# Conformer block on one core: 56 of 69 chunk transposes by DMA transposes inside SBUF

## The chip, the cores and the metric

The kernel runs on one core of a Trainium2 chip. The metric is the device time of one execution in microseconds (us), the median of several runs. In the text, PE is TensorE (its matmuls; PEld its weight loads), ACT ScalarE, DVE VectorE, POOL GpSimd, and SP the engine that issues most of the DMAs.

## The reference

Two sequences of 4000 tokens, 144 features each, in bfloat16, go through one Conformer block:

```python
def reference(x, w_ff1a, w_ff1b, w_qkv, w_o, w_pw1, dw, w_pw2, w_ff2a, w_ff2b):
    h = _layernorm(x, axis=-1)
    h = _silu(h @ w_ff1a) @ w_ff1b                    # 144 -> 576 -> 144
    x = x + 0.5 * h
    h = _layernorm(x, axis=-1)
    qkv = h @ w_qkv                                   # 4 heads of 36
    ...
    p = _softmax(scores, axis=-1)                     # 4000 x 4000 for each head
    att = jnp.einsum('bhqk,bhkd->bhqd', p, v)
    ...
    x = x + att @ w_o
    h = _layernorm(x, axis=-1)
    h = h @ w_pw1                                     # a, b: 144 each
    h = a * _sigmoid(b)
    ...                                               # depthwise convolution over 5 tokens
    x = x + _silu(c) @ w_pw2
    h = _layernorm(x, axis=-1)
    h = _silu(h @ w_ff2a) @ w_ff2b
    x = x + 0.5 * h
    return _layernorm(x, axis=-1)
```

## The kernel before

The 8000 tokens are cut into 16 chunks of 500, eight for each sequence, and a chunk into four blocks of 125. `X` holds all tokens in SBUF with tokens on the partitions. The attention of a chunk runs over the keys in tiles of 64: PE makes scores from `QT` and `KT` into PSUM, an exponential turns them into `PT`, and PE multiplies `PT` with `VA` into an accumulator. ACT makes 802 exponentials of 128x1000; for 190 further tiles DVE makes the exponential by integer arithmetic (two `PT<-PS` of 128x500 each, then three steps on `PT`).

Beside the attention run the other stages of each chunk: feed-forward 1 (`ff1`), projections to q, k and v (`pre2`), output projection and gate (`post1`), convolution and feed-forward 2 (`post2`). They need the chunk with features on the partitions. The layer norm (`ln`) is computed token by token: `bn_stats` on DVE, a power and four subtract-and-multiply steps on POOL, into a buffer `XN`. The attention's result is put by DVE into a buffer `AN` (`epilogue`). `transp` (and `transp_q` for the projections) brings such a buffer into the transposed `XT` (or `XTQ`), from which PE's matmuls read.

Of these chunk transposes 69 go the long way (`blocks`): DVE transposes all 32x32 blocks of the buffer, seen as pairs of bfloat16 in one float32, in place. SP issues four DMAs that write the buffer to a DRAM tensor `rows`, waits for their landing, and issues two DMAs that read it back so that the blocks come to stand in place (features 0 to 127, then 128 to 143). Because two blocks of tokens travel as a pair, `XN` and `AN` are written interleaved, and the matmuls read `XT` with a step of two elements. 41 of the 69 start from `XN` and go to `XT`, 15 from `AN` to `XT`, and 13 from `XN` to `XTQ`. The first and last chunks, where latency counts, are transposed on PE instead (`calm`).

The order of each engine's instructions is written out: a planner in the kernel walks through all work with fixed costs (the arguments `cost` and `lat`) and gives a first order, `PLACES` says which PSUM banks a tile takes, and `ORDER`, a string for each engine, says by how many places each step is moved from there. `Rec.reorder` applies it; `Rec.finish` works out the semaphore waits. Each engine then works through its own list in order, so an instruction that waits holds up those behind it. SP's list holds the loads of `X`, the stores of the result, and the DMAs of the transposes. All instructions are issued from one helper line, 398, which is why the profile shows that line everywhere.

Of the kernel before, what the change touches and what calls it, by code (L numbers as in the profile page):

```python
# [8 lines left out]
F32 = mybir.dt.float32  # L9
# [30 lines left out]
        "PPPPPPQOQOPPPPPRPNPPQQQQLPPQORPNPRPTMORNNVO~OLNOMrMMNPMMNNNOMNNNOPLMQMMMNNPMMNSMNLMMOOPNSOMQMSPNOPU["  # L40
        "OMNRMOPPQIRMSNPNePNOOOcNNNNNNNNNOOLbNLOOQNSH]MMOLOMPMMOOOVPNOOOOPPPTOOOTPMUQMSLNNQQNQOQQNPPPPPTPPROK"
        "PPPPPPPPPPPP`PPPQKVPPKPPMPPRPUPPPROQQQRZOQQQRRKQRRSJPRRRRRRRWSZRNYUR~NHQ@R[KEGOOOPPPPKQOPPSPPSLPQMTP"
        "PPLQQQMPPPQVPPQOX_PTOPPCRTQQRGSQIQQSQRNV8OOQNNVSNOOLOPUUNN_MMWLNNRMMMMOOOPPPPPPQQNPPRSNRSSSORRVTR[OR"
        "AKQ@PPLOOQQNPPPPPUOOOOOPQOPPPPPUOOOOQRPLU`NNNXMMPNLQMNLZRNL`MN_YLLMK`KMNLILNQJMOOOPNYOPNOOOQNNZ^NNNN"
        "OOPNQNQOYP]CNNNNOMPMSO[NKOOQNVMPMMN`NbYMMMMNOMNIcLLNL[MMMNNQNRMJQLLROQSPLRNOQOPUQOMPQMPPRPVPLQOMQNPQ"
        "QQQSKPQSQKQQQQJPPPPPWQQSPKKQQUPPPSWPQRPQAVPPPQCVPQRPWHSYPHSOPQYPQEPQCPRZUPPSOOHDPR^OKOOOOPNOOOO^NOQN"
        "NOOOSNNNNS[NNNdRMNRKYNJWJNNNNNNGOOPP^YNNNNOMNNNNRNNPPPVROOLOOPPRZNNOOOOOPNOSOPNRPSMOOPQOQWNRPRLLNSZP"
        "NPQOIOQOTPPPRPQ]P^USPMMQIQKQQ8QTQQGMRRTQQKRRRRGLRSOMRPQQQJQQRPVP[OOOQEROO^IOQLNOOPPTTOMNQ[FOQNPPSPPM"
        "HPQOQQUPLOPNVPNOOSQNLUOOPNOXPPPLTQNLMPPPQOPPTOOPTPLOOQRNOPPPQOVPNOOOORZOP[PPMOOFRZOL[ROQKQTUBOKNFPPP"
        "_OOOOOOPNOOOOWNNVNNXMNTKMNOMZQOSLNOMSPSLLTPMOOUOPNOOTQOMOPPPQOPPPQOPPPTTQOSQSSSSNEEPQOPTPTMOMORSNNOP"  # L50
        "ROYPQOPQ^NPNPQOPAOOOOOSOOOPPPQQNPPPPPPXOOOOOOOaNPPPLOOOPUMOOOO[IOOPSOOQNPHPSWOOPPPPQGPPPPQQQMPPQQNPQ"
        "O_OOOPZOOOPI_NNNNZOPEOQWP^HKPHSJOLNOO`VPMRJOM^J`MPNKUNLUGNLJQNRIOPPRXOMOOOOPXMOPPMOOOPWOOPPPTKNOOPPP"
        "PPPPPPPQRPSYSQNQYZPRRRADIOXQGVOPJOORPIPPRRSSMR]MHOOQQQVRKNHPLPPPPPPPPPPRZQSQRRbHSGNQGPPQRRGLPQKQQQQJ"
        "QOQRPMQOPPQOSQNRMTROTNPXQQQEPJOQNPRPN_OPPPLRSOPLPPPGPPPSeOMPPQRJZPKLNNNN`NOKOVJNNNNcM`LMMMNNN]MNL]LL"
        "LLLLTWLXKMMVNQ_LMOPPQQ>MOOOTOMRbMMOOOOOTOOOQZIOPJMOOcOMPPT[PRORPEVHOPYCJQOQQGMOQQNQWNQNPPLSP_OaOOOPN"
        "PDPPPLOHPPQLPPPPQOTPNWNPPPWJNPPP`OIOPPPPPPPUQOELRP^TTQOZUPPCGOPQDJPPPPPPRPQWPRURPMFQQ_RPXDPQJLPNOJPN"
        "PPPPPSPPQ`PPTQQRERPQIQTNDPTPPJOPQQNPPUOPPSLPMPPRPQQRPJP[RNQQLaRJQSS[IQMGQQRPCZJPQOPQTPP@RPIPPPPQQQSS"
        "VXUQGNTQSSETDS`OQSCJQQdLOINQMRLLZMNSMMMMZLWPK]JMNLMTLNNNNVN`NNNNNROOPPJQOPLRPRMOQQRPLPXQQQRPTUQHFPQJ"
        "PPPPPPSPROUSPPTLPUOCOPNQOPROTWPRWRPVRZOY^YEOOPPMQ:;QDQQQQQQQQQEQQQMQOROVSMOTTQLVHROTRGNTVPHRPTRaJSQE"
        "QRSKNRNOQOPWQO=OOPNYOOOQNNOO]QOL_PNRO^NOUIPNK_MMW>MMMZMMMM]MMQLMMSNNOMOPPSOVNNPNXNPQOKQOQLQQQQUPPPHO"  # L60
        "QORPQMQOPQQSQOUVWNWMNOKOAOQOPPPPZWNNNOOLNNR^MNVNOMNNNNPSMN]NTNNNNNaNNNOQLN[RNOMRNHMSOSNPQGPQOPRXRPQW"
        "KOHOPPQYPPZPQRCO[I^NORFNNIZMMMNOWLNNNQMNRORRO_KPNOOOYNNNNNNOU^NSUHNKOJNOSOOQRJUPROTYMHNNURNNTMIPNQOU"
        "OOV[MNLNNNPYTNeJLNORNNGOO[]NNNNIQLMRLNRWOPUOO]OM`QO;LSOLO]JOJPRLLMRUNZMOVR[NPDOT^OOOFOSTOMNOSbPQLPRS"
        "_MORR_NPP^OHCNNNOZOWL~NHLMMNNNSOOXNOQQNSSOIVKPNPN]NOOOOOPPVOOOITNPPLPPQOWPPMRPNTKOOTNOPUMOOOQN`OOOPN"
        "OOPPPLOZOQQMPIQO^YROQQRLENO_PNPPPTQNNOROOSVO]QMNRNOPWTNOMNSOPQXbOOOQ[NO~NCdIMMMMMMMfbKMMMQMMJLMPLMUM"
        "MMNL^TR^JSLJQJUKPNLHQMPP`UNNNNOMOOOOPNOOPPPPQQNPQQQMUQQMSOPTQOPTPQUNQSPSQ<TRSSVEQQQHQQFPPPPPQSPMYTOL"
        "NNTMNNNP^[NOMNNQMMOLNN]PNOOR[OPKQN_ZLNESMOOKHOM[NPPLPNOOPPMQSTMNPQQQQRSQRRTCQVNGRNOMTTTMMNUPPQHNQSPM"
        "YVTQKLLSSOIJPSSPTMKORNOQOPPPPPPSORNSMRNRRRNQQRPFRPQQQQQQRPFQO"
    ),
    "act": (  # L70
        "PPPPPPPPPPPPPRSNNOSOOOPPPPPPPUPNOXNNOOOOOQNPPPPPPPPPROOPPQOPPPQOPPPPPPQQNPPPPPPPPPPPPPPPPPPPPPPPPPQO"
        "PPPPPPPPPPPPPPPPPPPPPPPPPPPPPPPPPPPPPPPPPPPPPPPPPPPPPPPPPPPPPPPPPPPPPPPPQOROSNOOPPPPPPPPPPPPPPPPPPPP"
        "PPPPPPPPPPPPPQOPPPPPPPPPPPPPPPPPPPPPPPPPQOPPQOPPPPPPPPPPPPPPPPPPPPPPPPPPPPPPPPPPPPPPPPPPPPPPPPPPPPPP"
        "PPPPPPPPPPPPPPPPPPPPPPPPPPPPPPPPPPPPPPPPPPPPPPPPPPPPPPPPPPPPPPPPPPPPPPPPPPPPPPPPPPPPPQOPPPPPPPPPPPPP"
        "PPPPPPPPPPPPPPPPPPPPPPPPPPPPPPQOPPQOPPPPPPPPPPPPPPPPPPPPPPPPPPPPPPPPPPPPPPPPPPPPROOPPQOPPPPPPPPPPPPP"
        "PPPPPPPPPPPPPPPPPPQOPPPPPPPPPPPPPPPPPPPPPPPPPQOQOPPPPPPPPPPPPPPPPPPPPPPPPPPPPPPPPPPPPPPPPPPPPPPPPPPP"
        "PPPPPPPPTOPNOPPPPPPPPPPPPPPPPPPPPPPPPPPPPPPPPPPPPPPPPPPPPPPPPPPPPPPPPPPQOPPPPQOPPPPPPPPPPPPPPPPPPPPP"
        "PPPPPPPPPPPPPPPPPPPPPPPPPPPPPPPPPPPPPPPROOPPQQNPPPPPPPPPPPPPPPPPPQOPPPPPPPQOPPPPPPPPPPPPPPPPPPPPPPPP"
        "PPPPPQOPPPPPPPPPPPPPPPPPROOPPPPPPPPPPPPPPPPPQOPPPPPPPPPPPPQOPPPPPPPPPPPPPPPPPPPPPPPPPPPPPPPPPPPPPPPP"
        "PQOPPPPPPPPPPPPQOPPPPPPPPPPPPPPPPPPPPPPPPPPPPPPPPPPPPPPPPPPPPPPPPPPPPPPPPPPQOPPPPPPPPPPPPPPPPPPPPPPP"  # L80
        "PPPPPPPPPPPPPPPPPPPPPPPPPPPPPPPPPQOSPNRNOQOUQNPMOPPPRORNQNPPPPPPQOROQQMPPPPPPQOPPPWORNNNOO"
    ),
    "dve": (
        "PPROQQQLPPPUUNNNNSMUNNPNOQOSPNSUMOPLOPTPNPNPPQQQQQQQQHPVPRPLPLPPPRSSNRNQVPUOODNUMPNPNPPQSPMXNOOQNNOO"
        "PPPPPPPSOOOPPQOPPPPPPPPPPPPPPPPQOQOPPPPPPROQQMQOQOPPQORSQMQQQQQRPQWQRPQLPQQQVQQQSUKTQ2KMPQQQRRORPQQR"
        "RRTQQRTTPP;RPQBPPSOOORPNSOPRPQKQOPPPPPPcPQcQQQQTPPERPDLDNRNRNQQQRFQNQQNQOPQOPPPQOPPPPPPPPPPPPPPPQQTM"
        "PPRPQQQQUQOQUQQQSQRVGPPPPSPPRPQQ/PQOPPSPPQQKPPPPPQOPPPPQOPPPPPROOPQQNROQNPPPPQOPQOQQNPPPQTQOPQRPSPRR"
        "NSPPRPQQQ;QOPPPPPPPPPPPROOQOPSOOOPQOROOUSUOOQSQHRGOPPPPROOPPQRPMQRNQNQOPPPPPPPPPPQOPRPRPQKQOPQQQRPQQ"
        "QQQWROOPQO?PPPPPPPPQOPSOPQePPROOPPEOPNOPNOOOOOQNPPPPPROOPPPPRPRRRRJQKPPQOPPPPPPPPPPPQOPPPYOOPNPRMSMR"
        "LQMPPQOPPPPPPPPPPPPPPPPPQOROOPROOPPPPPPPPQOPQOQOPPROOTOOOOQOSOOOPROQNPPPPPPPPPPPQSPPLQOPPPROOPPPPPPP"  # L90
        "PPPQOPPPPPPPPPPQOPPPPPQOPPPPPPPQQVPLTPMOLPPRPNPQOPPRRNNPROQNPPPPPPPPPPQOQOQORORNOPROOPPPQQNPPPPQOPQR"
        "NOPQOPPPPPSPNOQQNQOPQOPPPPPQQQMPPPPPPPQOPPPQOQRPMROQQMPPQOPSPNOPPUOOOOOWOOOOOOOPPQOPPQQQQRPRPQGPPPPP"
        "PPPPPPQOPPPPUOOOPNPQOSOOSNOSNZQMPLOPNOOOPPPPPPQQNQOQOPPPPQOQOPPPRUOUQOUIOJOOPPPQOPPPPUOOOOOPPPQOROQT"
        "QOPJQOPPPPPPPQQQMPQOPPQRNTNTNNNQNQOPQOROQNPPQOPPPPPPSPNOTOOOOPPPQOQQUPVQOTHPNIQOVOPPMPQMPTOPPRLTNOOO"
        "PPPPPPUOOOOOPQOPPSPSQSQSQUSTEOELQOPPPPPPPSOPNPPROOVOOPNOOPPROOVOOPNOOPQRPUQQQVRUQUPCKPDPPPPQOPPPPQOP"
        "QOQOSPNOhQOPPPPPHOPNOPPQOROQNGOOPPPQOQOPQOPRPNPPPPQOPPPPPROTPPLQRULVOUOJPNJPPQOQOPRPQMPPPPPPPPQQQQQK"
        "QRNRNORPNUOUP[LNKPMRNRNLNQSSMRMRPKQOQQNQOWPPMQOXOPRPNSOWNCPNORNRTTPJSQMSPPQRZOROQQQQTPUHOPRO4PPPPPPQ"
        "QQRLRPQLPPPPPPPPPQOQQQMPPPPPQQQMPPPPPPPPPQQQSLTRPSQJQQQQQRTOPPRPRSQSQRRTQUPQTDO/OPS]NSMOLNQQNLOVQUPU"
        "OKHPLRRNNPPPQOPQRPQQQQVQOPQORSOP?PPPPPPPPPPPPRORPQQRPWQQNPTPUPUKOO<OPQOROQQMPQOPQQNPQQSPTQNPHPPROOQS"
        "NPQULPNOORROQRPJPPSOOORO]SOSNPRWQQXPTRERGRRTTUXRTRSBSSSSSSSSAT@S&NNPPPPPPPPPPQO"  # L100
    ),
    "pool": (
        "PPPPPPRPNPPPROOPPPSOOOPPPPPQQNPQOPPPYOOOOO[NNNR`NNJOMSMMOMOXOOLNOOUORLOMROQQQRPSIOOPPSOOOPQRNOPPPTOO"
        "PNPPPPVOOPNOQNPPPRPQM"
    ),
    "sp": (
        "PPPPPPPPQOPPPPPPPPPPPPPPSOTNNOOPPPQOPPPROQNPPPPPPPPPPPPPQOPPQOQOPPPPPPPPPPPPPPQOPPPPPVOPNSNNQMPPPQOP"
        "ROYNOOOPNOOUNTNOMNPPPSOOOPPPPPPPPPPPPPQOQOPPPPQQN"
    ),
# [16 lines left out]
    "2405240524052020420442045205420524052405240524052042505240524052402505423042302420340342034203420340"  # L126
    "2342042034203420243024202430243024034202340243204303420240240334024204302430243024302340134013413412"
    "0412041201412042041204024012412140214021401241205042304231514236404512412361021452243051351241353250"
    "213024014452502542036410"
)  # L130


# [1973 lines left out]
```

## Time and profile before

| | |
|---|---|
| median of 3 runs | 881.04 us (880.92 to 881.92) |
| span of the profiled execution | 880.5 us |
| the median over that span | 0.54 us |
| PE busy | 851.5 us (97%), 11419 matmuls |
| ACT busy | 849.6 us (96%), 1098 instructions |
| DVE busy | 822.7 us (93%), 1812 instructions |
| POOL busy | 300.4 us (34%), 584 instructions |
| DMA | 28.80 MB; the main queue takes 13.8% of the 16 DMA engines' time |

The profile is of one execution. A group is named by what its instructions write and read, output first (`XT<-rows`); with the number of instructions come their busy time, the mean of one in ns, and the idle time of the engine ahead of them with what ended it. DMA issues stand under SPq. Records of neighbouring instructions of one engine overlap by about 0.07 to 0.2 us, so the time from start to start is shorter than the mean that a group shows.

### The profile page before, as it was taken

The page shows a single profiled execution, that of the slowest core. Times are in us where ns is not written, and L with a number is a line of the kernel's source. Part 1 is how long each engine was busy: PE and PEld are TensorE (multiplying, and loading weights), DVE is VectorE, ACT ScalarE, POOL GpSimd, SP SyncE. Part 2 cuts the span into 40 slices and gives each one's busy share as a digit, 9 for nine tenths or more (in the row PEclk, how much of TensorE's full clock was granted, in tenths as well). Part 3 has the DMA queues.
Part 4 walks back from the last instruction along what each step waited for, and adds up shares of the span by engine and source line. Part 5 has one row for each costly group of instructions (what it writes and reads, how often), then busy time and mean ns, then how long its engine had stood idle before and what let it go on. Part 6 is the DMA issues. An engine that isn't in the chain of part 4 may idle for free.

```text
span 880.5 us, 27000 instructions
## 1 busy us (share of the span) xinstructions
PE 851.5 (97%) x11419; PEld 380.2 (43%) x11419; DVE 822.7 (93%) x1812; ACT 849.6 (96%) x1098; POOL 300.4 (34%) x584
## 2 busy tenths in 40 slices
PE   8998999999999999999999999999999999999996
PEld 6543433344444443443444444344443433444366
DVE  7977999999999999999989999899999999999987
ACT  6799999999999999999999999999999999999986
POOL 7770331431336130252111813522513404032434
PEclk9999999999999999999999999999999999999999
DMA  3221001220221110212001120110110011001111
GB/s 100 44 55 38 16 18 36 62 51 16 40 49 38 23 38 22 45 24 45 16 9 30 36 44 23 23 26 20 43 31 18 21 37 20 17 12 36 27 27 33
DMA packets 114351, 28.80 MB, mean 33 GB/s; under 512 B 101090, under 2 KB 114230, under 8 KB 114230
## 3 DMA queue, kind: packets, MB, share of 16 engines
q1 hardware_dynamic: 112646, 26.39, 13.8%
q8 instruction: 89, 1.46, 0.7%
q10 hardware_dynamic: 1584, 0.69, 0.3%
q14 instruction: 32, 0.26, 0.1%
HBM read 13.44 MB, written 13.61 MB: 31 GB/s over the span
## 4 chain that ended last, share of the span: by engine, by line
ACT 46%; PE 33%; DVE 17%; POOL 2%; DMA 1%; issue 1%; SPq 1%; POOLq 0%; DVEq 0%
ACT PT L398 42%; PE PS L398 33%; DVE PT L398 7%; ACT TH L398 4%; DVE HT L398 2%; DVE ST L398 2%; DVE X L398 2%; DVE XN L398 2%; POOL RS L398 1%; POOL XN L398 1%; DVE KT L398 1%; DVE QT L398 1%; DVE AN L398 1%; SPq L398 1%; DMA rows<-XN 0%
## 5 line engine op out<-in xcount | busy, mean ns | idle before, releaser
L398 ACT ACTIVATE PT<-PS 128x1000 bf16<-128x1000 f32 (+1 forms) x818 | 757.2, 1074 | 4.1 <-PE PS L398 2.4
L398 PE MATMUL PS<-QT,KT 64*64 64x500 bf16 x3968 | 425.7, 385 | 13.0 <-ACT PT L398 5.2
L398 PE MATMUL PS<-PT,VA 64*37 64x500 bf16 x4728 | 411.5, 372 | 1.8 <-DVE QT L398 0.7
L398 DVE TENSOR_SCALAR PT<-PS 128x500 int16<-128x500 f32 x380 | 250.1, 668 | 5.8 <-PE PS L398 3.9
L398 PEld LDWEIGHTS PS<-QT,KT 64*64 64x64 bf16 x3968 | 123.4, 104 | 236.8 <-ACT PT L398 137.1
L398 POOL TENSOR_SCALAR RS<-ST 125x4 f32<-125x4 f32 x130 | 37.0, 284 | 482.2 <-DVE ST L398 475.6
L398 PEld LDWEIGHTS PS<-PT,VA 64*37 64x37 bf16 x4728 | 141.4, 96 | 96.2 <-DVE PT L398 18.7
L398 DVE TENSOR_SCALAR PT<-PT 128x1000 uint16<-128x1000 uint16 x380 | 154.5, 418 | 2.1 <-PE PS L398 0.8
L398 POOL TENSOR_SCALAR XN<-X,RS 125x144 bf16<-125x144 bf16 x260 | 150.4, 610 | 13.1 <-DMA out_dram<-XN 6.4
L398 DVE TENSOR_TENSOR PT<-PT 128x1000 bf16<-128x1000 bf16 x190 | 128.8, 679 | 1.3
L398 ACT ACTIVATE TH<-PS 128x500 bf16<-128x500 f32 (+3 forms) x194 | 107.3, 575 | 7.4 <-PE PS L398 6.5
L398 POOL TENSOR_TENSOR RS<-RS,NHALF 125x4 f32<-125x4 f32 (+1 forms) x93 | 91.7, 989 | 33.1 <-DVE RS L398 27.3
L398 DVE SCALAR_TENSOR_TENSOR HT<-TH,PS 128x500 bf16<-128x500 bf16 (+1 forms) x135 | 81.2, 615 | 12.8 <-ACT TH L398 12.0
L398 PE MATMUL PS<-XT,WA 80*128 80x500 bf16 (+5 forms) x288 | 74.5, 365 | 2.2 <-DMA XT<-rows 0.9
L398 DVE BATCH_NORM_STATS2 ST<-X 125x6 f32<-125x288 bf16 x160 | 65.7, 447 | 2.8 <-DMA X<-in_x_dram 2.7
L398 DVE SCALAR_TENSOR_TENSOR X<-PS,X 125x288 bf16<-125x288 f32 (+1 forms) x128 | 56.6, 449 | 6.5 <-PE PS L398 5.2
L398 PE MATMUL PS<-WB,HT 128*125 128x144 bf16 (+1 forms) x640 | 52.4, 230 | 0.7 <-ACT HT L398 0.5
L398 PEld LDWEIGHTS PS<-WB,HT 128*125 128x125 bf16 (+1 forms) x640 | 44.3, 136 | 14.5 <-issue 3.8
L398 PEld LDWEIGHTS PS<-XT,WA 128*128 128x128 bf16 (+1 forms) x288 | 21.2, 97 | 38.8 <-issue 10.6
L398 PE MATMUL PS<-U,DG 128*128 128x250 bf16 (+6 forms) x204 | 29.6, 264 | 0.0
L398 DVE STREAM_TRANSPOSE XN<-XN 128x320 f32<-128x320 f32 x54 | 27.0, 500 | 1.0 <-POOL XN L398 1.0
L398 POOL COPY U<-U 128x2 bf16<-128x2 bf16 (+1 forms) x54 | 9.2, 209 | 46.3 <-DVE U L398 46.3
(95 smaller groups left out, 522.6 us busy)
## 6 DMA issues: line engine op xcount, KB each, us to landing
rows<-XN SPq DMA_DIRECT2D x216, 40.0 KB, 2.0
XT<-rows SPq DMA_DIRECT2D x56, 128.0 KB, 2.0
rows<-AN SPq DMA_DIRECT2D x60, 40.0 KB, 2.0
X<-in_x_dram SPq DMA_DIRECT2D x15, 140.6 KB
XTQ<-rows SPq DMA_DIRECT2D x26, 70.3 KB
out_dram<-XN SPq DMA_DIRECT2D x13, 140.6 KB
XT<-rows SPq DMA_DIRECT2D x56, 16.0 KB, 1.9
out_dram<-XN SPq DMA_DIRECT2D x3, 70.3 KB
```

The source lines that it names most:

```text
L398: ins = getattr(eng, o.name)(*o.a, **o.k)
```

## The change

For the 56 transposes into `XT`, the block transpose on DVE, the writes to DRAM and the reads back are gone. SP issues four `dma_start_transpose` instead, one for each block of 125 tokens. Each takes 128 partitions by 256 columns of `XN` or `AN` and writes them transposed to 128 partitions by 2x128 in `XT`. A block has 144 columns, so the rest of the 256 are columns of the next blocks; they end in rows of `XT` whose weights are zero. `XN` and `AN` grow from 640 to 688 columns, and are no longer interleaved for these transposes; `XT` is read densely, and its clearing at the start is dropped. The 13 transposes into `XTQ` stay as they are.

The planner still plans the removed instructions, as `ghost` ones with their old costs; `reorder` takes them out and passes their dependences on. `ORDER` and `PLACES` are new throughout. The numbers of exponentials on ACT and on DVE, and of all matmuls, are the same in both orders.

```diff
 def transp(u, an, s, bs, inter, dma, rows=TB):
...
         if dma and s not in xt_set:
             xt_set.add(s)
-            op("pool", "memset", XT[0:LP, s, 1, :, :], 0.0, w=wk, cost=0.5)
+            op("pool", "ghost", w=wk, cost=0.5)
         if dma:
-            yield from blocks((ANF if an else XNF)[:, u, :], key, s,
-                              [(XTF[0:128, s, 0, :, :], 0, 128, 128, 0.43, T_LAT), (XTF[0:16, s, 1, :, :], 128, D, 128, 0.43, T_LAT)], f"t{s}", wk)
+            yield need("dve")
+            op("dve", "ghost", r=[key], w=[key], cost=c_dve(320))
+            yield need("sp")
+            first = None
+            for i in range(NB):
+                args = "sp", "dma_start_transpose", XT[:, s, :, i, :], (ANS if an else XNS)[:, u, i * D:i * D + 256]
+                if first is None:
+                    first = op(*args, q=f"t{s}", r=[key], w=[("DT", s)] + wk, cost=W_COST, lat=W_LAT)
+                else:
+                    R.more(first, [key], [("DT", s)] + wk, *args, q=f"t{s}", cost=W_COST, lat=W_LAT)
+            yield need("sp")
+            first = op("sp", "ghost", q=f"g{s}", r=[("DT", s)], w=wk, cost=0.43, lat=T_LAT)
+            R.more(first, [("DT", s)], wk, "sp", "ghost", q=f"g{s}", cost=0.43, lat=T_LAT)
+            more_x()
             return
...
 def xt(s, k, i0, i1=None, rows=TB):
         if i1 is None:
-            return XTJ[0:KK[k], s, k, i0 // 2, 0:rows, i0 % 2] if x_inter[s] else XT[0:KK[k], s, k, i0, 0:rows]
-        if x_inter[s]:
-            return XTJ[0:KK[k], s, k, i0 // 2:i1 // 2, 0:rows, :].rearrange("p g n j -> p g j n")
+            return XT[0:KK[k], s, k, i0, 0:rows]
         return XT[0:KK[k], s, k, i0:i1, 0:rows].rearrange("p (g j) n -> p g j n", j=2)
...
 def ln_tr(c, s, bs, e=False): ...
 def ln_trq(c, bs):
         inter = len(bs) == NB and not calm(c)
-        u = yield from ln(c, bs, inter=inter)
+        u = yield from ln(c, bs, inter=inter, pairs=inter)
```

`W_COST, W_LAT = 0.655, 1.8` and `T_LAT = 2.0` are unchanged lines of the kernel.

## The prediction

> **What bounds the kernel now.** I read the page's head first, then the chain, the groups with their forms kept apart, the windows, the DMA issues, SP's timeline and the waits.
>
> ```profile
> PE 851.5 (97%) x11419; PEld 380.2 (43%) x11419; DVE 822.7 (93%) x1812; ACT 849.6 (96%) x1098; POOL 300.4 (34%) x584
> ```
>
> ```profile
> ACT 46%; PE 33%; DVE 17%; POOL 2%; DMA 1%; issue 1%; SPq 1%; POOLq 0%; DVEq 0%
> ```
>
> Three engines are nearly full, and the chain runs through ACT, PE and DVE; DMA, which the change works on, holds 1% of it.
>
> ```profile
> L398 ACT ACTIVATE PT<-PS 128x1000 bf16<-128x1000 f32 x802 | 749.3, 1082 | 4.0 <-PE PS L398 2.4
> ...
> L398 PE MATMUL PS<-XT,WA 128*128 128x500 bf16 x112 | 44.2, 395 | 2.0 <-DMA XT<-rows 0.9 <-ACT PT L398 0.9
> ...
> L398 DVE STREAM_TRANSPOSE XN<-XN 128x320 f32<-128x320 f32 x54 | 27.0, 500 | 1.0 <-POOL XN L398 1.0
> ...
> L398 PE MATMUL PS<-XTQ,WQ 72*128 72x500 bf16 x60 | 17.9, 379 | 0.1
> ```
>
> The exponentials on ACT are most of its work. Their records overlap: they start 0.884 us apart where nothing delays them.
>
> ```profile
> 0.00:22.00 22.00, 18.47 (x221) 15.09 (x225) 15.90 (x63) 13.93 (x30) 15.66 (x43) 1.00 0.40 100
> 22.00:44.00 22.00, 20.03 (x207) 11.67 (x207) 21.02 (x55) 16.15 (x30) 16.89 (x34) 1.00 0.21 44
> ...
> 638.00:660.00 22.00, 21.80 (x306) 9.43 (x306) 21.96 (x46) 21.99 (x29) 3.52 (x7) 1.00 0.15 31
> ...
> 858.00:880.00 22.00, 15.85 (x195) 13.85 (x193) 17.79 (x70) 13.56 (x35) 9.61 (x13) 0.94 0.11 33
> ```
>
> The columns after the length are PE, PEld, DVE, ACT, POOL. In the middle (638 to 660) ACT is busy 21.99 of 22 us. Summed over all such windows, ACT is idle 15.7 us before 88 us, 4.0 us from 88 to 836, and about 11 us after that. So ACT's work bounds the kernel between its ends, and the change leaves ACT's instructions as they are: 802 large exponentials in both orders, 380 halves on DVE in both.
>
> ```profile
> rows<-XN SPq DMA_DIRECT2D x216, 40.0 KB, 2.0
> XT<-rows SPq DMA_DIRECT2D x56, 128.0 KB, 2.0
> ```
>
> ```profile
> 672.63 2.55 SPq L398 DMA_DIRECT2D rows<-AN  x4
> 676.61 0.82 SPq L398 DMA_DIRECT2D XT<-rows  x2
> ```
>
> The last number of a DMA row is us from issue to landing. One chunk's way: four writes issued in 2.55 us, the last lands 2.0 us after its issue, the two reads start 3.98 us after the first write, take 0.82 us to issue and land. Over all 56 chunks, from the first write's issue to the last read's landing, the median is 6.8 us. With DVE's block transpose ahead (0.43 us to the next start, its record 0.50, the 15 of AN alike) it is 7.3 us.
>
> ```profile
> PEld PS L398 <- ACT PT L398: 148.3, 406, 1.1
> ...
> PEld PS L398 <- DMA XT<-rows: 4.7, 6, 1.4
> ```
>
> The columns are us in total, times, and the longest. PE's weight loads wait mostly for ACT and DVE, which are full, and little for XT. That is not from wide margins: from a chunk's landing to the first matmul that waits for it I read, 56 times, a median of 2.2 us; five are under 0.5 us, ten under 1.0, sixteen under 1.5.
>
> **The change, part by part.** Everything is set against the profiled span of 880.5 us; the median of the runs shown, 881.04, lies 0.54 above it, and I add that back.
>
> DVE loses 41 + 15 = 56 block transposes: 56 x 0.50 = 28 us of records, 56 x 0.43 = 24 us of pace. Where ACT is at 21.99 of 22 us this shortens nothing; it is cover for DVE's waits. Taken as 0; at most, by DVE's 17% of the chain, 0.17 x 24 = 4.1 us gained.
>
> XT loses its pairs of interleaved blocks, so 284 matmuls of 500 columns read it densely. By the rows above 395 goes to 379 ns for 128 rows; with the other rows (388 for XT,WA at 80 rows, 397 and 389 for XT,WP) the sum is 112x16 + 112x9 + 30x18 + 30x10 ns = 3.6 us of PE. By PE's 33% of the chain that is 1.2 us at most; taken as 0, for PE waits for ACT anyhow.
>
> POOL loses five clears of XT (519 ns each, 2.6 us, all near the start), and gains 48 columns in each XN clear (630 ns for 640, so under 0.3 us for all five) and 192 in AN's (2227 ns for 2560: 0.2 us). POOL is 34% busy; its waits for DVE hide this. Taken as 0, at most 2 us in the first 60.
>
> SP loses 224 writes at 0.64 and 56 pairs of reads at 0.82 us, 189 us of issue, and the 56 waits of a read for its write, behind which later stores, loads and XTQ transfers stood. It gains 224 transposing DMAs. The 13 XTQ chunks keep the old way. SP was idle most of the time, so only the latency counts.
>
> The price of a transposing DMA is not in the trace. Bounds for the issue: from 0.39 us (the 128-row read of XT) to 0.84 us (XTQ's read, 1.68 us for two). Bounds for the landing: 1.9 to 3.1 us from issue (median of the smallest read, slow tail of the writes). The way of one chunk is three issues and a landing: 3x0.39 + 1.9 = 3.1 to 3x0.84 + 3.1 = 5.6 us, in place of 7.3. I take the dear issue, since each instruction moves 64 KB and spreads every row over 128 partitions, and 2.5 us for the landing, midway: 3x0.84 + 2.5 = 5.0 us.
>
> A shorter way would be a gain only if a reader stood waiting. But the order was laid anew, and the diff gives each of the four DMAs a cost of 0.655 and a latency of 1.8 us: 4x0.655 + 1.8 = 4.4 us. I take it that readers were drawn up against about that figure. The order of PE's instructions bears this out in part: between the last WP2Z matmul of a chunk and its first XT,WA matmul, PE's work, priced at the trace's pace, shrinks from at least 14.0 to at least 12.0 us, for single chunks by 1.5 to 2.6. From the last matmul on IDF to the first on WO it is 10.1 before and 9.7 after, so that group keeps its room.
>
> If margins over the assumed way are spread as they are now, a way that is longer by x costs the sum over the 56 margins of what x exceeds them. At x = 5.0 - 4.4 = 0.6 us: the six smallest margins (0.05, 0.09, 0.16, 0.26, 0.28, 0.57) give 2.2 us. At x = 1.2 (way 5.6): 8 us. At or below 4.4: 0. PE is in order, so matmuls of scores stand behind a waiting XT matmul, and ACT behind these; I count each stall in full.
>
> Sum: 880.5 + 2.2 + 0.5 = 883.2 us, rounded to 883.5 since another order also shifts stalls that I can't see.
>
> **The rivals.** *Faster:* the freed time reaches the chain. 4.1 (DVE) + 1.2 (PE) = 5.3 us off: 875.7. For it: DVE is at 99% in several windows, and PE's weight loads wait 68.9 us for its PT. Against it: ACT has only 4.0 us of idle time between 88 and 836, and no block transpose is a step of the chain that stands out. It needs a way of 4.4 us or less and a landing of 2.0 us. The Trainium skill, "Advanced Engine Details and Errata", section "X-Bar Transpose (TRN2)", says that such DMAs are as fast as regular ones; by that x is 0 and this rival or the next one holds. No run so far shows it.
>
> *No change:* the way is short enough and nothing else moves: 881.0.
>
> *Much slower, the transposes go one after another:* if each holds the path until it has landed (0.65 issue + 2.0 landing from the rows above), four take 10.6 us, 3.3 more than the old 7.3. By the margins of now that is 66 us: 881 + 66 = 947; with readers drawn closer it is more, with half of that overlap about 900. Decisive point: the old 7.3 us, an issue of 1.6 us with a landing of 2.5. For it: nothing in the trace shows such a DMA. Against it: the ordinary ones overlap, issued 0.64 apart with a landing of 2.0. The Trainium skill, "VectorE: DVE Perf Modes", section "The three transpose paths", speaks for this rival: it gives 1309 ns for 128x128 through the DMA crossbar, and each instruction here holds two of these. By that figure four instructions are an estimated 10.5 us, and the sum would be about 945 us.
>
> **How the numbers follow.** Late readers, my forecast, 883 to 891: 0.42. Faster: 0.27. No change: 0.15. One after another, 900 and above: 0.16. The range reaches down to the faster rival and a little below, 874, and up to 900, beyond the 889 of the upper bounds; it leaves out the last rival. 0.2% (1.8 us) is about what a measurement of this kernel can tell from no change: slower is 0.42 + 0.16 = 0.58, same 0.15, faster 0.27. Within my forecast alone the range is 882.8 to 891.
>
> **What would show it.** In the profile after: 56 fewer block transposes, DVE near 795 us, ACT still near 850; XT,WA matmuls at 380 ns; a group of 224 transposing DMAs whose row gives the landing, and SP's timeline the issue. Right if four issues and a landing come to 4.5 to 5.6 us and PE's waits for XT rise from 5.6 us (4.7 + 0.9) by 2 to 10. Wrong on the slow side if the issue is over 1.6 us; wrong on the fast side if ACT's idle time before 88 us or in the middle falls by more than 2 us while PE's waits for XT stay.

## The result, and the profile after

The changed kernel takes 894.9 us (median of 4 runs, 894.47 to 896.67); the kernel before takes 881.48 us beside it (4 runs, 880.92 to 882.27). The ratio is 1.0156, with a 95% interval of 1.0144 to 1.0168: slower by 13.4 us, where the forecast said 2.5. The profiled execution has a span of 894.9 us and took 896.67, so it lies 1.8 us above the median; its span is 14.4 us longer than that of before. Executions that were disturbed are left out of the comparisons; one of them is the profile of e2_old_order, which is why that kernel appears a second time as e10.

The head of the page and the chain that ended last, in the changed kernel (all instructions now come from line 414):

```profile
PE 847.5 (95%) x11419; PEld 385.5 (43%) x11419; DVE 810.2 (91%) x1756; ACT 850.0 (95%) x1098; POOL 292.7 (33%) x579
...
ACT 37%; PE 31%; DVE 15%; SPq 7%; DMA 5%; POOL 3%; issue 1%; DVEq 0%; POOLq 0%
```

ACT's work is what it was (850.0 us, 849.6 before). In the chain SP's issue has gone from 1% to 7% and DMA from 1% to 5%, in ACT's place (46% to 37%).

Where the time is lost shows in a cut into start, middle and end. First before, then after; columns as in the prediction: length, then PE, PEld, DVE, ACT, POOL busy, granted TensorE clock, DMA share, GB/s.

```profile
0.00:88.00 88.00, 79.78 (x957) 43.16 (x957) 69.29 (x181) 72.32 (x114) 48.12 (x105) 1.00 0.26 59
88.00:836.00 748.00, 733.83 (x10016) 308.94 (x10014) 716.41 (x1513) 743.99 (x913) 235.97 (x448) 1.00 0.14 30
```

```profile
0.00:88.00 88.00, 79.03 (x965) 43.90 (x969) 69.85 (x177) 72.94 (x114) 42.58 (x98) 1.00 0.25 58
88.00:836.00 748.00, 717.76 (x9828) 308.05 (x9816) 691.31 (x1435) 730.64 (x898) 220.18 (x423) 0.99 0.12 26
```

Between 88 and 836 us ACT was idle for 748 - 743.99 = 4.0 us before and is idle for 748 - 730.64 = 17.4 us now. These 13.4 us are nearly all of the 14.4; the start has not changed (15.7 and 15.1 us idle).

PE's and ACT's waits in the changed kernel (us in total, times, longest), then, by groups, the matmuls that read `XT` and what is left of the block transposes:

```profile
PEld PS L414 <- DMA XT<-XN: 17.3, 11, 4.6
ACT TH L414 <- PE PS L414: 14.0, 13, 4.4
PE PS L414 <- DMA XT<-XN: 11.3, 8, 4.2
```

```profile
L414 PE MATMUL PS<-XT,WA 128*128 128x500 bf16 x112 | 43.2, 385 | 13.8 <-DMA XT<-XN 10.8 <-DVE PT L414 1.3 <-ACT PT L414 0.6
...
L414 DVE STREAM_TRANSPOSE XN<-XN 128x320 f32<-128x320 f32 x13 | 6.5, 500 | 0.0
```

The matmuls' row of before, which the prediction adds to the 4.7 us of the weight loads:

```profile
PE PS L398 <- DMA XT<-rows: 0.9, 1, 0.9
```

PE's waits for `XT` are 17.3 + 11.3 = 28.6 us, where they were 4.7 + 0.9 = 5.6. One stop can stand in both rows, once for the weight load and once for the matmul behind it (4.6 and 4.2 are the same one), so these sums compare the two kernels and are not lost time. The matmuls alone stood for 11.3 us. The block transposes on DVE are down to the 13 of `XTQ`, as the change says.

The price of the new instruction, from the DMA issues, from SP's records for `XT` (ns: shortest, median, longest), and from the timeline of SP from 634 to 636 us (start, duration):

```profile
XT<-XN SPq DMA_TRANSPOSE x164, 2.4
...
XT<-AN SPq DMA_TRANSPOSE x60, 2.4
```

```profile
L414 SPq DMA_TRANSPOSE XT<-XN x164: 1167/1247/3481, 21.1 to 863.4; - x164
```

```profile
633.55 1.25 SPq L414 DMA_TRANSPOSE XT<-AN  x1
634.84 1.25 SPq L414 DMA_TRANSPOSE XT<-XN  x1
```

One issue holds SP for 1.25 us, and the next starts 1.29 us after it (634.84 - 633.55); the landing comes 2.4 us after the issue. A chunk's way is 3x1.29 + 2.4 = 6.3 us. That is a good chunk: from the first issue to the last landing, the median of the 44 chunks whose landing the trace tells is 6.7 us. The old way took 6.8 by the same measure, so little more than DVE's block transpose ahead of it has been saved. From start to start the 224 issues take 224 x 1.29 = 289 us of SP, where the removed ones took 189.

The largest single loss, in the timelines of POOL, SP and PE (the bracket is PE's idle time ahead and what ended it):

```profile
625.95 2.54 POOL L414 TENSOR_SCALAR XN<-X,RS 125x144 bf16<-125x144 bf16 x4
```

```profile
628.88 5.92 SPq L414 DMA_TRANSPOSE XT<-AN  x4
634.84 12.46 SPq L414 DMA_TRANSPOSE XT<-XN  x8
```

```profile
641.15 0.84 PE L414 MATMUL PS<-XT,WA 128*128 128x500 bf16 x2 [4.23 <-DMA XT<-XN]
```

POOL has finished the chunk's `XN` at 628.49. At 628.88 SP starts four transposes of another chunk's `AN`, which stand ahead in its list and hold it until 634.80. The chunk's own four (the first half of the x8) follow at 634.84, the last lands at 641.1, and PE has stood still for 4.23 us. So 6.4 of the 12.6 us from `XN` to `XT` were a wait for SP. By the dependences that the kernel works out and the times in the trace, 22 of the 56 chunks stood more than 1 us on SP after their data were ready. In the kernel before it was 13, so standing in line is not new, but there is more of it.

What follows that stop, in the windows around it:

```profile
637.00:641.00 4.00, 0.00 (x0) 0.00 (x0) 2.27 (x6) 0.67 (x1) 3.21 (x7) 1.00 0.24 49
641.00:643.00 2.00, 1.85 (x14) 0.47 (x14) 0.35 (x1) 0.97 (x2) 0.24 (x1) 0.59 0.20 39
643.00:646.00 3.00, 3.00 (x25) 0.76 (x22) 1.92 (x4) 2.24 (x4) 0.00 (x0) 0.70 0.12 23
646.00:650.00 4.00, 3.90 (x59) 1.73 (x57) 3.16 (x8) 4.00 (x7) 0.00 (x0) 1.00 0.16 33
```

PE is back at 641, but the granted clock falls to 0.59 and 0.70: in the five us from 641 to 646 PE does 39 matmuls, in the four from 646 to 650 it does 59. A stop is paid twice: ACT was idle for 3.3 us from 637 to 641, and for another 1.8 us from 641 to 646.

### The profile page after: what moved, and what is told of

Same layout as the page of the kernel before. It is cut to its first block, busy times and chain, and to the rows that moved or that the text cites. A ratio compares the mean times of both kernels' runs of the same rounds, so it can differ in the third digit from the quotient of the medians.

```text
span 894.9 us, 26867 instructions
## 1 busy us (share of the span) xinstructions
PE 847.5 (95%) x11419; PEld 385.5 (43%) x11419; DVE 810.2 (91%) x1756; ACT 850.0 (95%) x1098; POOL 292.7 (33%) x579
## 4 chain that ended last, share of the span: by engine, by line
ACT 37%; PE 31%; DVE 15%; SPq 7%; DMA 5%; POOL 3%; issue 1%; DVEq 0%; POOLq 0%
ACT PT L414 33%; PE PS L414 31%; SPq L414 7%; DVE PT L414 7%; ACT TH L414 3%; DMA XT<-XN 2%; DVE ST L414 2%; POOL RS L414 1%; DMA XTQ<-rows 1%; DVE X L414 1%; DVE HT L414 1%; POOL XN L414 1%; DVE XN L414 1%; DMA rows<-XN 1%; DMA out_dram<-XN 1%
## 5 line engine op out<-in xcount | busy, mean ns | idle before, releaser
L414 PE MATMUL PS<-PT,VA 64*37 64x500 bf16 x4728 | 404.6, 375 | 0.9 <-DVE QT L414 0.4
L414 DVE TENSOR_SCALAR PT<-PS 128x500 int16<-128x500 f32 x380 | 251.0, 671 | 12.7 <-PE PS L414 10.6
L414 PEld LDWEIGHTS PS<-QT,KT 64*64 64x64 bf16 x3968 | 125.4, 104 | 240.4 <-ACT PT L414 136.7
L414 PEld LDWEIGHTS PS<-PT,VA 64*37 64x37 bf16 x4728 | 142.7, 96 | 89.0 <-issue 13.9
L414 DVE TENSOR_SCALAR PT<-PT 128x1000 uint16<-128x1000 uint16 x380 | 156.3, 425 | 2.5 <-PE PS L414 0.6
L414 POOL TENSOR_SCALAR XN<-X,RS 125x144 bf16<-125x144 bf16 x260 | 143.6, 569 | 8.3 <-DMA out_dram<-XN 1.6
L414 ACT ACTIVATE TH<-PS 128x500 bf16<-128x500 f32 (+3 forms) x194 | 104.4, 556 | 14.9 <-PE PS L414 14.0
L414 PEld LDWEIGHTS PS<-WB,HT 128*125 128x125 bf16 (+1 forms) x640 | 44.5, 136 | 13.9 <-issue 3.6
L414 PE MATMUL PS<-U,DG 128*128 128x250 bf16 (+7 forms) x204 | 28.2, 263 | 0.1
L414 PE MATMUL PS<-IDF,QT 128*125 128x128 f32 x128 | 22.9, 303 | 0.4 <-DVE QT L414 0.2
```

The source lines that it names most:

```text
L414: ins = getattr(eng, o.name)(*o.a, **o.k)
```

## The experiments

The theory after the result: the issue of a transposing DMA costs SP 1.29 us from start to start instead of the 0.84 taken, and the new order leaves its readers no room for that. Rivals: the order itself is worse, whatever the DMAs cost; or the DMAs disturb other engines.

**Half as wide.** Each DMA moves 128 columns instead of 256.

```diff
-                args = "sp", "dma_start_transpose", XT[:, s, :, i, :], (ANS if an else XNS)[:, u, i * D:i * D + 256]
+                args = "sp", "dma_start_transpose", XT[:, s, 0, i, :], (ANS if an else XNS)[:, u, i * D:i * D + 128]
```

> The order of the changed kernel, but each transposing DMA takes 128 columns instead of 256, so it moves half as much; features 128 to 143 of these chunks are left out, their rows of XT are cleared once. Issue price (the new order was laid for a way of about 4.4 us and gets 3 x 1.29 + 2.39 = 6.3): if the price goes by the amount moved, the issue falls to about 0.65 us, the way to 4.3 us, PE's waits for XT (28.6 us after) fall under 8 us and the time to 880 to 884 us. The new order itself is the loss: the waits go the same way, but the time stays at 890 to 895 us. A fixed price for each instruction: issue and time stay as they are, 893 to 896 us.

Measured: 891.82 us, ratio 1.0106 (1.0084 to 1.0129). Its records on SP:

```profile
L414 SPq DMA_TRANSPOSE XT<-XN x164: 1094/1232/3245, 21.4 to 856.0; - x164
```

Half the data, and the issue is 1232 ns instead of 1247. The price does not go by what is moved, and most of the loss stays (10.1 of 13.4 us). The time is below the 893 to 896 us that a fixed price was expected to give. What the 3 us are is not shown; in the profiled runs PE lost 3.4 us to half clock between 88 and 836 us here, and 6.8 in the changed kernel (see the clock after a stop).

**Twice as many.** Each DMA is cut in two of 128 columns, so the same data takes eight. The second of each pair is planned at no cost (not shown), so that the order stays.

```diff
-            for i in range(NB):
-                args = "sp", "dma_start_transpose", XT[:, s, :, i, :], (ANS if an else XNS)[:, u, i * D:i * D + 256]
+            for i, k in [(i, k) for i in range(NB) for k in range(2)]:
+                args = "sp", "dma_start_transpose", XT[:, s, k, i, :], (ANS if an else XNS)[:, u, i * D + 128 * k:i * D + 128 * k + 128]
```

> The changed kernel and its order, each transposing DMA cut into two of 128 columns, so eight for a chunk that move the same. Price by amount moved: issue about 0.65 us each, way and time unchanged, 892 to 898 us. Price fixed for each instruction: issue 1.29 us each, the way about 11.4 us, SP busy 10 us for each chunk, 1000 us or more.

Measured: 1080.08 us, ratio 1.224 (1.2211 to 1.2268). The chain and PE's largest waits:

```profile
SPq 35%; PE 21%; ACT 14%; DVE 14%; DMA 6%; POOL 5%; issue 2%; DVEq 0%; POOLq 0%
```

```profile
PEld PS L414 <- DMA XT<-XN: 124.3, 24, 14.8
```

448 issues of 1.23 us hold SP for 552 us, and SP's issue is now the largest share of the chain. The mean granted clock is 0.913.

**One instead of four.** One DMA of 512 columns for each chunk, in the new order. As in the first experiment, POOL clears the rows of `XT` that nothing fills (not shown).

```diff
-            for i in range(NB):
-                args = "sp", "dma_start_transpose", XT[:, s, :, i, :], (ANS if an else XNS)[:, u, i * D:i * D + 256]
...
+            op("sp", "dma_start_transpose", XT[:, s, 0, :, :], (ANS if an else XNS)[:, u, 0:512], q=f"t{s}", r=[key], w=[("DT", s)] + wk, cost=4 * W_COST, lat=W_LAT)
```

> The changed kernel and its order, one transposing DMA of 512 columns for a chunk in place of four of 256; it moves half of what these move, puts other columns than the right ones into the first rows of XT and leaves features 128 to 143 out. Price by amount moved: issue about 2.6 us, way 2.6 + 1.1 = 3.7 to 5 us, time 880 to 885 us. Fixed price: issue 1.3 us, way about 2.5 to 3.7 us, time 880 to 883 us; the two differ in the issue.

Measured: 881.86 us, ratio 0.9998 (0.9985 to 1.001).

```profile
L414 SPq DMA_TRANSPOSE XT<-XN x41: 1188/1192/1308, 21.2 to 843.5; - x41
```

Four times the columns of e1 in one instruction, and still 1192 ns. With three of four issues gone, 13.0 of the 13.4 us are gone too, and no wait of PE for `XT` is left in its trace. So the price goes by the number of instructions, and most of the loss goes with it. That the DMAs disturb other engines is not borne out: half of the data (e1) kept most of the loss, and half of the data in a quarter of the instructions (here) lost nearly all of it.

**The order of before.** The four DMAs of 256 columns, with the strings `ORDER` and `PLACES` of the kernel before (the strings are left out here).

```diff
-    ORDER, PLACES of the changed kernel
+    ORDER, PLACES of the kernel before
```

> The changed kernel with its 256-column transposing DMAs, but with every engine's order and the PSUM places of the kernel before (the removed instructions simply missing). Issue price against readers drawn close: the way is again 6.3 us, under the 7.3 us that this order was laid for, so PE's waits for XT are under 8 us and the time is 879 to 884 us. The transposing DMAs disturb other work wherever they stand (contention, SP blocked for 5.1 us for each chunk): 888 to 895 us. Freed DVE time reaches the chain: 874 to 878 us.

Measured: 880.66 us, ratio 0.9981 (0.9971 to 0.999). The same kernel again, for its trace:

> The same kernel as the changed one with the order of before, run again for its trace. If each transposing DMA costs SP about 1.2 to 1.3 us whatever it moves, and the order of before has room for a way of 7.3 us, then four issues and a landing (6.3 us) fit: PE's waits for XT stay below 3 us, against 28.6 in the changed kernel, and the time is 880 to 882. If the loss were something that the DMAs do to other engines (SBUF traffic, stores held up), PE's waits would be small but ACT or DVE would show the 13 us, and the time would be near 890.

Measured: 880.55 us, ratio 0.9984 (0.9975 to 0.9993). The price of the instruction is the same, and the middle is full again:

```profile
L414 SPq DMA_TRANSPOSE XT<-XN x164: 1167/1247/2438, 20.7 to 846.8; - x164
```

```profile
88.00:836.00 748.00, 733.65 (x10046) 309.47 (x10038) 702.08 (x1465) 744.40 (x915) 230.91 (x448) 1.00 0.13 27
```

ACT is idle for 3.6 us there, and no PE wait for `XT` from a DMA shows among the waits. The dear DMAs stand in line on SP here too: 23 of the 56 chunks stand over 1 us after their data are ready. The readers of this order, which were laid for a way of 7.3 us, have the room for it. This complete version beats both kernels, by 0.16% over the one before. It also answers the rival that the DMAs disturb other engines: they are the same 224 of 256 columns as in the changed kernel.

**The order of before, one DMA.** Both edits together.

> Order of before, and one transposing DMA of 512 columns for each chunk in place of four; features 128 to 143 are left out. The way of a chunk is one landing, 2.4 us, in place of 7.3 us. If a shorter way and 24 us less of DVE were worth something by themselves (the faster rival), the time falls to 876 or below. If the order of before leaves its margins unused, as I think, nothing more is gained than with four DMAs: 879 to 881.

Measured: 878.47 us, ratio 0.9971 (0.9959 to 0.9982), closest to the expectation of 879 to 881, and 0.5 us below it. Four kernels now form a square (medians in us; the kernel before took 881.5 to 881.8 beside them):

| | four DMAs | one DMA |
|---|---|---|
| new order | 894.9 | 881.9 |
| order of before | 880.6 | 878.5 |

Four issues in place of one cost 2.1 us in the order of before and 13.0 in the new one. The new order costs 3.4 us by itself, even with the shortest way. (By the ratios to the kernel before the three are 1.1, 13.9 and 2.4 us.) So the order is a part of the loss, but a small one; most of it is the order and the price together.

The line on SP can be compared along the same square: 22 chunks stand over 1 us in the changed kernel and 13 in e4, 23 in e10 and 12 in e11. Four issues in place of one add some ten chunks in either order. What differs is the room: with one DMA, the tightest chunk of the new order has 2.7 us between its landing and its reader, and the tightest of the old order 5.5. In the changed kernel PE stood still until the landing of eight chunks, 12.2 us in sum (1.3 of it stand under DVE in the waits). Four of the eight, with 8.1 us, had stood 1.7 to 4.6 us longer on SP than the same chunks of e4. The other four, with 4.1 us, had not, and there the longer way alone used up the room, or nearly.

**DVE's relief alone.** The kernel before, its way through DRAM kept, with the 56 block transposes into `XT` cut to a tenth.

```diff
-        op("dve", "transpose", v, v, r=[key], w=[key], cost=c_dve(320))
+        op("dve", "transpose", v[:, 0:(320 if q.startswith("tq") else 32)], v[:, 0:(320 if q.startswith("tq") else 32)], r=[key], w=[key], cost=c_dve(320))
```

> The kernel before with its way through DRAM, but the 56 block transposes into XT work on 32 of 320 columns each, so that the blocks reach XT not transposed within themselves. DVE is relieved of some 20 us and nothing else changes. If freed DVE time reaches the chain by DVE's 17% share, the time falls by 3 to 4 us, to about 877.5. If it is cover only, the fall is under 1 us.

Measured: 879.77 us, ratio 0.9983 (0.9974 to 0.9991), a gain of 0.8 to 2.3 us: between the two expectations. DVE's busy time fell by 12.0 us (822.7 to 810.7).

**The clock after a stop.** No run was made for this; it is read from the traces in hand. These are all of PE's idle times of 0.9 us or more between 88 and 836 us, with the mean granted clock of the 10 us behind each:

| kernel | idle ahead of PE, us (clock behind it) |
|---|---|
| before, e10, e11, e12 | none |
| changed | 2.33 (0.66), 0.97 (1.00), 1.07 (1.00), 1.34 (1.00), 0.97 (1.00), 1.85 (0.83), 4.23 (0.83) |
| e1, half as wide | 2.33 (1.00), 0.96 (1.00), 1.37 (1.00), 0.97 (1.00), 3.68 (0.70) |
| e4, one DMA | 2.33 (0.83), 0.97 (1.00) |

The stops under 1.4 us left the clock alone; of the six from 1.85 us up, five were followed by half clock. Summed over windows of 2 us, the changed kernel lost (1 - clock) x time = 6.8 us of PE between 88 and 836, before and e10 none. The stop of 2.33 us waits for DVE's `QT` and is there in e4 as well, so it belongs to the new order; those of 1.85 and 4.23 wait for transposes. That the clock falls because of the stop is read from their sequence, and not tested by a run of its own.

The Trainium skill, "TensorE: Matmul & The Clock Gate", section "HAM oscillation — how this bites in real kernels", asks that PE should not be idle for more than about 3.4 us. The trace agrees that a stop is followed by half clock, but here 1.85 us was enough, and one of 2.33 us went without.

## Why the prediction was right or wrong

**Right:** the direction and its mechanism, late readers of `XT` in an order drawn for a shorter way. Of ACT's 14.0 us of further idle time 13.4 are in the middle; DVE's and PE's savings were nothing that could pay for it. The landing, taken as 2.5 us, is 2.4.

**Not right: the size,** +13.4 us against +2.5. The time lies in the range of 874 to 900 only because this was drawn wider than the forecast's own 882.8 to 891. The signs that the prediction set for itself fail too: the way is 6.3 us and not 4.5 to 5.6, and PE's waits for `XT` rose by 23.0 us and not by 2 to 10.

**The failed step: the issue.** It was taken as 0.84 us, the dear end of the bounds from rows of ordinary DMAs; it is 1.29. The way is 6.3 us instead of 5.0, and the excess over 4.4 is 1.9 us instead of 0.6. The reason given for the dear end ("each instruction moves 64 KB") was wrong as well: 128, 256 and 512 columns cost 1.23, 1.25 and 1.19. With 1.9 the prediction's own margins give at least 16 us (the six smallest 6x1.9 - 1.4 = 10.0, the four up to 1.0 at least 3.6, the six up to 1.5 at least 2.4), so 897 us or more. That this is near 894.9 is in part luck: the measured time also holds 3.4 us of the new order by itself, the line on SP and the half clock, of which these margins know nothing. The issue is still the term that was mis-sized, since with one DMA in place of four 13.0 us are gone. The upper bound of the issue should have gone past the rows of a different instruction.

**"SP was idle most of the time, so only the latency counts"** failed too. Chunks stood in line on SP before (13 of 56), and with 289 us of issue for the transposes 22 did. The chunk of the largest stop, 4.2 us, stood 6.4 us on SP; in e4 the same chunk stood 2.8, so 3.6 us of that stop came out of the line and not out of the chunk's own way.

**"I count each stall in full"** was too little for the long ones: the half clock behind three of them is another 6.8 us of PE.

**DVE near 795 us** was wrong: 810.2, and 804.7 in e10. Busy time is a union of records, and neighbouring records overlap, so the 28 us of records were at most 24 us of pace; why only 12.5 to 18 us of busy time went is not shown. On the path, DVE's term of 0 with a bound of 4.1 was near: e12 gives 1.9 by the medians, and 0.8 to 2.3 by its interval.

**The XT,WA matmuls** were to fall from 395 to 380 ns: 385 in the changed kernel, with the half clock in it, and 383 in e10.

**The rivals.** *Faster* needed a way of 4.4 us or less. In e11, with 2.4, it gives 2.6 us by the ratio (3.2 by the medians) of the 5.3 foreseen, so the mechanism exists at about half its size, and not in the new order. The rule of the Trainium skill behind it ("Advanced Engine Details and Errata", section "X-Bar Transpose (TRN2)", as fast as regular DMAs) about holds for the landing, 2.4 beside 2.0 us, and not for the issue, 1.29 beside 0.39 to 0.84. *One after another* foresaw 10.6 us for a chunk from the rows: the four landings overlap, so it did not come. The figure of the Trainium skill beside it (1309 ns for 128x128, "VectorE: DVE Perf Modes", section "The three transpose paths") is within 0.1 us of the measured price of an instruction. Here that is a price of the instruction, and not of each 128x128 in it. The point named as decisive, an issue of 1.6 us, was too high: the loss was there at 1.29, since the new order's room was smaller than the old 7.3 us and the line on SP came on top.

**Open:** why the new order is 3.4 us worse than the old one even with the shortest way, beyond its stop for `QT`. Not tried: all four blocks in one DMA with all of their features. It needs blocks 256 columns apart, which for nine buffers is 336 more columns or 6 KB for each partition; no run shows whether there is room. By e11 it would be worth an estimated 2 us over e10. Nor was an order laid anew for 1.29 us tried.

## What to carry to other kernels

Price an instruction that the trace doesn't hold by its number of issues as well as by its data, and bound it well beyond the rows of its nearest relatives; then ask what it makes of the queue that issues it, not only of its own latency. An order laid by hand or by search is only as good as the prices behind it: here the cheaper-looking way with a fitted order lost 1.6%, and the same way in an order laid for a slower one gained 0.2%. Count PE's stops by length: here half clock followed most of those from 1.85 us up and none up to 1.37, so a few long ones can cost more than many short ones of the same sum.

## What the hardware showed unexpectedly

A transposing DMA from SBUF to SBUF holds SP for about 1.2 us whether it moves 128 (1.23), 256 (1.25) or 512 columns (1.19), all of 128 partitions, and lands 2.4 to 2.6 us after its issue. After stops of 1.85, 2.33 and 4.23 us PE's granted clock was at half for parts of the next 10 us, with means of 0.83, 0.66 and 0.83, while stops up to 1.37 us left it at 1.00.
